# Attention, dense MLP and routed experts in one kernel: the routing's constants set up in eight pieces, and new pace numbers for the list that orders the work

## The chip, the cores and the metric

The kernel runs on one core of a Trainium2 chip. The metric is the device time of one execution in microseconds (us); less is better. Three executions of the kernel before took 875.04, 875.09 and 876.19 us, the median is 875.09 us.

## What is computed

The reference has three layers in a row, all in float32:

```python
# 1: attention with random features, 4 x 8 heads, 576 positions, 64 wide, 128 features
q_p, k_p = phi(q_s), phi(k_s)       # exp(x omega^T - |x|^2/2 - max) / sqrt(m)
kv, z = einsum('bhsm,bhsd->bhmd', k_p, v), sum(k_p, axis=2)
attn = (q_p @ kv) / (q_p @ z + 1e-6)
# 2: dense MLP, 2304 tokens x 512, hidden 2048
h = x @ w_in
x = (h - tanh(h)) @ w_out
# 3: eight experts, each token to one expert, at most 288 tokens an expert
logits = x @ w_gate                 # greedy assignment in order of the logits
out[mask] = maximum(x[mask] @ w1[e], 0) @ w2[e]
```

## The kernel before, in words

**Tiling.** The 2304 tokens are six blocks of 384. The dense MLP goes block by block; a block has 16 chunks of 128 hidden columns. A chunk is twelve matmuls into one PSUM bank (`chunk_ops`, L608 to L610: high and low parts of the float32 numbers multiplied in three products), a Square of the bank into `u` (L612, ScalarE), the polynomial for h - tanh(h) (L632 on ScalarE, L633 and L635 on VectorE), the split into high and low parts (`hidden_ops`, L303 and L308), and nine matmuls with the second weight matrix (`m2_ops`, L655). The ring of `u` has one buffer, that of the PSUM banks four.

**Attention** is cut into units (`unit_ops`): projections on TensorE (L433), a maximum on VectorE (L447), exponentials on ScalarE (L444), then either the sum over positions (L464) or the product with it (L486, L493, L506). 18 units run ahead of the MLP, the other 54 are spread over the first four blocks. `x_ops` (L548 to L556, and helpers L303 and L308) turns a finished token tile into the MLP's operand.

**Weights** come as 64-bit floats. `weight_ops` loads one 128 x 512 piece (L337, SyncE queue), takes it apart into a float32 in three VectorE operations (L338, L340, L342), rounds it to the high part on ScalarE, subtracts for the low part on GpSimd or VectorE (`low`, L308) and stores the low part in HBM (L351). There are 16 pieces of the first matrix ("wi") and 16 of the second ("wo"); the MLP loads the low parts again (`split_ops`, L569, tiles iL and oL, three buffers each).

**What sets the order.** All operations are handed to a planner (`Plan`) while the program is built. Each has an engine, a duration as the list believes it, the operations that it depends on, buffers of rings, and a due time (`plan.at` plus a lag). The planner plays the program through in its own time: of all that is ready it issues what can begin first, and among what can begin at the same time what is due first. So each engine gets its instructions in one fixed order. Due times, unless an operation is marked `early=False`, hold nothing back; they only decide between things that compete. An operation on the engine "-" costs the list nothing and runs its Python function when it is its turn: whatever instructions that function emits stand in the engines' queues at that place.

The due times come from a few pace numbers: T_MLP (due time of the first chunk), SB and SU (a block's length is SB plus SU for each attention unit in it), DUE0 and DUE1 (how far after the block's start its first attention unit is due, and how much of its end is left without), WI0, WI1 and WO0 (pieces of the weights), LEADX, LEADI and LEADO (how far ahead the MLP's operand and the two low parts are due). `low_ops` prepares low parts of the experts' weights in the fifth block with a pace of its own.

**The routing's constants** are made by `r_setup` (L956 to L1026): 14 index patterns by iota on GpSimd (L962 and L1002) and 31 short operations on VectorE (L972 to L1025). They are used only after the fifth block, by the routing. Before, one "-" operation emits all of them once the first chunk's Square (`flags[:1]`) has been issued.

Two small transfers, the zero row of the MLP's output (L1487) and the gate's weights (L1490), are on the SyncE queue near the start.

Of the kernel before, what the change touches and what calls it, by code (L numbers as in the profile page):

```python
# [8 lines left out]
F32 = mybir.dt.float32  # L9
# [180 lines left out]
def tile_kernel(ctx, tc, q, k, v, omega, w_in, w_out, w_gate, w_gate_t, w1, w2, out, dbg=None):  # L190
    nc = tc.nc
# [4 lines left out]
    P = 128  # L196
# [5 lines left out]
    NF = DFF // P  # L202
    E = w_gate.shape[1]
    BLK = 384
    NBLK = NT // BLK
    TPB = BLK // P
# [25 lines left out]
    ms = dram.tile([NT + 1, DM], F32, name="ms")  # L232
# [14 lines left out]
    wg = consts.tile([P, NC, P // NC], F32, name="wg")  # L247
# [19 lines left out]
    plan = Plan()  # L267
# [44 lines left out]
    bwg = Buf(None)  # L312
# [16 lines left out]
    def weight_ops(kind, f, rings, masked=None):  # L329
        raw, w, lw = (Buf(r) for r in rings)  # L330
        if kind == "wo" and not masked:
# [3 lines left out]
        V = nc.vector  # L335
        bits = lambda: w.t.bitcast(U32)
        plan.op(SP, 0.47, lambda e: nc.sync.dma_start(pair(raw), src64[kind][f]), w=[raw], nbytes=P * DM * 8)  # L337
        plan.op(DVE, 0.52, lambda e: V.tensor_scalar(  # L338
            bits(), raw.t[:, :, 1], 5, 2, op0=OP.logical_shift_left, op1=OP.logical_shift_right), r=[raw], w=[w], lag=5.0)
        plan.op(DVE, 0.66, lambda e: V.scalar_tensor_tensor(  # L340
            bits(), raw.t[:, :, 1], 0xC0000000, bits(), op0=OP.bitwise_and, op1=OP.bitwise_or), r=[raw, w], w=[w], lag=5.4)
        plan.op(DVE, 0.73, lambda e: V.scalar_tensor_tensor(  # L342
            bits(), raw.t[:, :, 0], 29, bits(), op0=OP.logical_shift_right, op1=OP.bitwise_or), r=[raw, w], w=[w], lag=6.0)
# [426 lines left out]
    HINT = NBLK * NF - 6  # L770
    LAG2, LEADX, LEADI, LEADO = 10.4, 15, 5.43, 4.91

    def mlp_ops(start, step, general=False):
# [4 lines left out]
        for j in range(NBLK - 1):  # L778
            for i in range(j, j + 1 if j < NBLK - 2 else NBLK):
                x[i] = Buf(xHr), Buf(xLr)  # L780
                for t in range(TPB):
                    plan.at = start[j] + (3.0 if i > j else -LEADX) + 1.5 * t
                    if i == j > 0 and not general:
                        plan.at = max(x_due[i * TPB + t] + 9.0, start[j - 1] + LEADX)
                    x_ops(i, t, *x[i], general)
# [170 lines left out]
    def r_setup():  # L956
# [3 lines left out]
        def iota(name, shape, pattern, base=0, cm=0):  # L960
            x = c.tile(shape, I32, name=name)
            nc.gpsimd.iota(x, pattern=pattern, base=base, channel_multiplier=cm)  # L962
            return x
# [3 lines left out]
        for i, wd in enumerate(WIDTH):  # L967
# [5 lines left out]
            t["bits"].append((x, n, sh))  # L973

        x, n, sh = t["bits"][0]
        f0 = c.tile([P, n], I32, name="thr0")
# [4 lines left out]
        nc.vector.tensor_tensor(f0, f0, z, op=OP.bitwise_xor)  # L981
        t["thr0"] = f0
        de = iota("dei", [P, E], [[-1, E]], base=E)
        t["desc"] = c.tile([P, E], F32, name="desc")
# [4 lines left out]
        nc.vector.tensor_copy(flat(t["jid"]), ji)  # L989

        pi = iota("pi", [P, 1], [[0, 1]], cm=1)
        pd = c.tile([P, 2], I32, name="pdig")
# [4 lines left out]
        nc.vector.tensor_copy(pf[:, 1:3], pd)  # L997
        nc.vector.tensor_scalar(pf[:, 3:4], pd[:, 1:2], 1.0 - P, float(P), op0=OP.mult, op1=OP.add)
        t["tri"] = c.tile([P, P], BF16, name="tri")
        nc.vector.tensor_scalar(t["tri"], jp, 0.0, None, op0=OP.is_gt)  # L1000
        sp = jp
        nc.gpsimd.iota(sp, pattern=[[0, P // LO], [1, LO]], base=0, channel_multiplier=0)  # L1002
        t["spread"] = c.tile([P, P], BF16, name="spread")
        nc.vector.tensor_scalar(t["spread"], sp, pf[:, 1:2], pf[:, 3:4], op0=OP.is_equal, op1=OP.mult)
        hm = iota("hmi", [P, NHI], [[1, NHI]])
        nc.vector.tensor_scalar(hm, hm, P // LO - 1, None, op0=OP.bitwise_and)
        t["hm"] = c.tile([P, NHI], F32, name="hm")
        nc.vector.tensor_scalar(t["hm"], hm, pf[:, 2:3], None, op0=OP.is_equal)
        t["rsel"] = c.tile([P, NG * P // LO], F32, name="rsel")
        nc.vector.memset(t["rsel"], 0.0)  # L1010
# [8 lines left out]
        nc.vector.memset(t["mfull"], 0.0)  # L1019
        nc.vector.memset(t["mfull"][:1], -1.0e6)  # L1020
        t["id8"] = c.tile([P, E], BF16, name="id8")
        nc.vector.tensor_copy(t["id8"], ident[:, :E])
        for name, n in (("d8", 1), ("r1", NHI)):
            t[name] = Buf(None, c.tile([P, n], BF16, name=name))
            nc.vector.memset(t[name].t, 0.0)  # L1025
        rt.update(t)  # L1026

    rings = {}
# [457 lines left out]
    plan.op(POOL, 0.3, lambda e: nc.gpsimd.memset(zero.t[:1].bitcast(F32), 0.0), w=[zero])  # L1486
    plan.op(SP, 0.47, lambda e: nc.sync.dma_start(ms[:1, :], zero.t[:1].bitcast(F32)), r=[zero])  # L1487
    plan.at = 30.0
    plan.op(POOL, 0.1, lambda e: nc.gpsimd.memset(wg, 0.0), w=[bwg])
    plan.op(SP, 0.47, lambda e: nc.sync.dma_start(wg[:, :, :E], w_gate.rearrange("(c p) e -> p c e", p=P)), w=[bwg])  # L1490
    units = attn_units()
    NEARLY = 18
    T_UNIT, T_MLP, DUE0, DUE1 = 2.2, 68.1, 4, 20


    SB, SU = 40.5, 1.95
    along = [16, 14, 14, 10, 0]
# [7 lines left out]
    for i, u in enumerate(units):  # L1505
        plan.at = due[i]
        unit_ops(*u, early=i < NEARLY)
        if i == NEARLY - 1:
            early_ops = plan.ops[n0:]
    WI0, WI1, WO0 = 4.51, 3.28, -1.5  # L1510
    for f in range(NF):
# [29 lines left out]

    low_ops(starts[-2], (NF * steps[-1] - 8.0) / (E * NPRE))
    plan.at = T_MLP
# [8 lines left out]
    plan.at = T_MLP + 100.0  # L1552
    plan.op("-", 0.0, lambda e: r_setup(), after=flags[:1])
    plan.op("-", 0.0, lambda e: tc.mark_branch_hint_location(
# [143 lines left out]
```

## Time and profile before

| | |
|---|---|
| median of three executions | 875.09 us |
| time of the profiled execution | 876.29 us |
| its span, first to last instruction | 874.5 us |
| around the span | 1.8 us |
| TensorE busy | 845.2 us (97% of the span) |
| VectorE busy | 652.2 us (75%) |
| ScalarE busy | 468.4 us (54%) |
| GpSimd busy | 247.0 us (28%) |
| mean granted clock of TensorE | 0.99 |

The profile shows one execution. Attention ahead of the MLP fills the first 50 us; the six MLP blocks follow up to some 535 us, then routing and experts. A wait of an engine is given with the work that ended it. The granted clock is 1.00 at 2.4 GHz and 0.50 at 1.2 GHz. TensorE's ends are modelled, so 100% busy doesn't say that every matmul ran at its shortest.

### The profile page before, as it was taken

To read this page: it belongs to the slowest core of one execution; us is meant where nothing else is said; L and a number is where in the kernel's file an instruction comes from. 1 tells how busy PE (TensorE), PEld (TensorE's weight loads), DVE (VectorE), ACT (ScalarE), POOL (GpSimd) and SP (SyncE) were. 2 spreads that over 40 slices of the span, in tenths; PEclk is the share of its full clock that TensorE was granted. 3 is DMA by queue.
4 is the path that set the end of the run, shared out by engine and by line. 5 is a ranking of instruction groups with operands and counts; after the bars stand their busy time and mean duration, and the time that the engine had idled before them with its cause. 6 is when DMAs were issued, how large, how long until landed. Compare 5 with 4: busy or idle time off the path is not lost. (4 is left out here: it accounts for less than half of the span.)

```text
span 874.5 us, 17508 instructions
## 1 busy us (share of the span) xinstructions
PE 845.2 (97%) x6158; PEld 754.0 (86%) x6158; DVE 652.2 (75%) x1933; ACT 468.4 (54%) x1018; POOL 247.0 (28%) x271
## 2 busy tenths in 40 slices
PE   8989999999999999999999998999999999999995
PEld 6878888888888888898988985777999999999995
DVE  5897999886677888797888866446887878877520
ACT  5875565654456554655457853014465555555621
POOL 1232433223352344344431024010132232231211
PEclk9999999999999999999999999999999999999998
DMA  8997878987457665743469874577889879779500
GB/s 248 330 299 245 281 239 264 291 273 240 126 177 215 183 198 190 240 125 109 134 213 335 278 257 155 172 246 252 262 204 295 277 200 277 264 182 339 199 28 28
DMA packets 103789, 193.94 MB, mean 222 GB/s; under 512 B 28305, under 2 KB 42257, under 8 KB 103698
## 3 DMA queue, kind: packets, MB, share of 16 engines
q1 hardware_dynamic: 98034, 173.92, 60.7%
q0 software_dynamic: 5664, 18.88, 9.0%
q8 instruction: 49, 0.80, 0.4%
q14 instruction: 42, 0.34, 0.1%
HBM read 149.64 MB, written 33.69 MB: 210 GB/s over the span
## 5 line engine op out<-in xcount | busy, mean ns | idle before, releaser
L608 PE MATMUL bk<-xH,wi 128*128 128x384 f32 x332 | 118.7, 358 | 1.9 <-DVE xt L506 1.1
L736 DVE SCALAR_TENSOR_TENSOR lw<-wf,raw 128x512 f32<-128x512 f32 x128 | 108.6, 848 | 5.4 <-POOL wf L733 4.0
L609 PE MATMUL bk<-xL,wi 128*128 128x384 f32 x332 | 112.1, 338 | 0.5 <-DVE xL L308 0.5
L610 PE MATMUL bk<-xH,iL 128*128 128x384 f32 x332 | 112.2, 338 | 0.0
L655 PE MATMUL acc<-wo,gL 128*128 128x512 f32 x282 | 111.2, 395 | 0.0
L308 POOL TENSOR_TENSOR gL<-s,gH 128x384 fp32r<-128x384 f32 x49 | 58.8, 1200 | 145.9 <-ACT gH L303 143.5
L655 PE MATMUL acc<-wo,gH 128*128 128x512 f32 x240 | 99.4, 415 | 0.0
L444 ACT ACTIVATE phi<-bk,nm 128x128 f32<-128x128 f32 x272 | 77.2, 384 | 35.4 <-DVE nm L447 35.0
L655 PE MATMUL acc<-oL,gH 128*128 128x512 f32 x240 | 95.0, 396 | 0.3 <-DVE oL L308 0.3
L733 POOL TENSOR_TENSOR wf<-oL,wo 128x512 f32<-128x512 f32 x48 | 66.6, 1389 | 64.5 <-DMA oL<-low_wo 54.3
L303 ACT ACTIVATE gH<-s 128x384 fp32r<-128x384 f32 x80 | 42.0, 525 | 62.5 <-DVE s L635 43.4
L633 DVE SCALAR_TENSOR_TENSOR s<-s,bk 128x384 f32<-128x384 f32 x83 | 45.5, 549 | 35.5 <-ACT s L632 35.2
L608 PEld LDWEIGHTS bk<-xH,wi 128*128 128x128 f32 x332 | 63.0, 190 | 9.8 <-issue 2.0
L609 PEld LDWEIGHTS bk<-xL,wi 128*128 128x128 f32 x332 | 63.1, 190 | 3.2 <-DVE xL L308 0.7
L655 PEld LDWEIGHTS acc<-wo,gL 128*128 128x128 f32 x282 | 53.0, 188 | 12.5 <-POOL gL L308 0.4
L612 ACT ACTIVATE u<-bk 128x384 f32<-128x384 f32 x80 | 39.2, 490 | 44.8 <-PE bk L610 43.3
L610 PEld LDWEIGHTS bk<-xH,iL 128*128 128x128 f32 x332 | 62.7, 189 | 0.0
L447 DVE TENSOR_REDUCE nm<-bk 128x4 f32<-128x512 f32 (+1 forms) x75 | 46.3, 631 | 10.7 <-PE bk L433 9.2
L635 DVE SCALAR_TENSOR_TENSOR s<-s,u 128x384 f32<-128x384 f32 x80 | 51.8, 648 | 1.3
L632 ACT ACTIVATE s<-u,qbias 128x384 f32<-128x384 f32 x80 | 49.4, 617 | 4.9 <-DVE gL L308 3.2
L655 PEld LDWEIGHTS acc<-wo,gH 128*128 128x128 f32 x240 | 45.2, 188 | 7.2 <-ACT xm L303 0.4
L655 PEld LDWEIGHTS acc<-oL,gH 128*128 128x128 f32 x240 | 45.2, 188 | 6.1 <-DVE oL L308 0.6
(417 smaller groups left out, 2325.1 us busy)
## 6 DMA issues: line engine op xcount, KB each, us to landing
r_wraw<-in_moe_w_dram SPq DMA_DIRECT2D x50, 512.0 KB
iL<-low_wi SPq DMA_DIRECT2D x80, 256.0 KB
oL<-low_wo SPq DMA_DIRECT2D x78, 256.0 KB
raw<-in_moe_w_in_dram SPq DMA_DIRECT2D x32, 512.0 KB
raw<-in_moe_w_out_dram SPq DMA_DIRECT2D x32, 512.0 KB
s_wraw<-in_moe_w_dram SPq DMA_DIRECT2D x14, 512.0 KB
dw<-in_moe_w_dram SPq DMA_DIRECT2D x13, 512.0 KB
w1l<-dw SPq DMA_DIRECT2D x13, 512.0 KB
```

What stands on the lines that cost most here:

```text
L308: (nc.gpsimd if e == POOL else nc.vector).tensor_tensor(out, in_, high.bitcast(F32), op=OP.subtract)
L444: nc.scalar.activation(ph.t[:, i0 + i, :], pj.t[:, i * M:(i + 1) * M], AF.Exp, bias=nmx.t[:, i0 + i:i0 + i + 1])
L447: plan.op(DVE, 0.1 + 0.125 * n, lambda e, pj=pj, i0=i0, n=n: V.tensor_reduce(nmx.t[:, i0:i0 + n], pj.t[:, :n * M].rearrange("p (i m) -> p ...
L608: nc.tensor.matmul(ph(), piece(iH, c), xH.t[:, c, :], start=(c == 0), stop=False)
L609: nc.tensor.matmul(ph(), piece(iH, c), xL.t[:, c, :], start=False, stop=False)
L610: nc.tensor.matmul(ph(), piece(iL, c), xH.t[:, c, :], start=False, stop=(c == NC - 1))
L632: plan.op(ACT, 0.52, lambda e: nc.scalar.activation(s.t, ut(), AF.Square, bias=qbias), r=[u], w=[s], lag=2.8)
L633: plan.op(DVE, 0.52, lambda e: V.scalar_tensor_tensor(s.t, s.t, QD, ph(), op0=OP.add, op1=OP.mult), r=[p, s], w=[s], lag=3.4)
L635: plan.op(DVE, 0.65, lambda e: V.scalar_tensor_tensor(s.t, s.t, QC, ut(), op0=OP.mult, op1=OP.mult), r=[u, s], w=[s], lag=4.0)
L655: nc.tensor.matmul(acc[t].t, (gL if k == 2 else gH).t[:, c], (oL if k == 1 else oH).t, start=(f == 0 and k == 0), stop=(f == end and k == ...
L733: plan.op(POOL, 1.45, lambda e: nc.gpsimd.tensor_tensor(w.t, lo.t.bitcast(F32), wo[:, f, :].bitcast(F32), op=OP.add), r=[lo, wbuf["wo", f] ...
L736: x_reads.append(plan.op(DVE, 0.9, lambda e, i=i: nc.vector.scalar_tensor_tensor(scratch.t.bitcast(F32), w.t, 1.0, half(rows[i // 2], i % ...
```

## The change

`r_setup` becomes a generator with eight yields. In place of the one "-" operation there are eight operations on VectorE, each believed to take 0.5 us, each after the one before it and after the Square of one of chunks 24 to 31 (the second half of the second block). Three durations of the conversion and the pace numbers get other values, and the two small transfers are not issued before their due times (60 and 30 us of the list's time).

```diff
 def weight_ops(...)
-        plan.op(DVE, 0.52, lambda e: V.tensor_scalar(
+        plan.op(DVE, 0.5, lambda e: V.tensor_scalar(
...
-        plan.op(DVE, 0.66, lambda e: V.scalar_tensor_tensor(
+        plan.op(DVE, 0.78, lambda e: V.scalar_tensor_tensor(
...
-        plan.op(DVE, 0.73, lambda e: V.scalar_tensor_tensor(
+        plan.op(DVE, 0.75, lambda e: V.scalar_tensor_tensor(
...
-    LAG2, LEADX, LEADI, LEADO = 10.4, 15, 5.43, 4.91
+    LAG2, LEADX, LEADI, LEADO = 10.4, 16.22, 0.85, 5.03
...
-                        plan.at = max(x_due[i * TPB + t] + 9.0, start[j - 1] + LEADX)
+                        plan.at = max(x_due[i * TPB + t] + 9.4, start[j - 1] + LEADX)
...
 def r_setup():
     (seven of the eight yields stand between these parts, the last at the end:)
     bits | thr0 | desc, i16, i18, jid | pf | tri, iota into jp | spread, hm | rsel to mfull | id8, d8, r1
...
-    plan.op(SP, 0.47, lambda e: nc.sync.dma_start(ms[:1, :], zero.t[:1].bitcast(F32)), r=[zero])
+    plan.op(SP, 0.47, lambda e: nc.sync.dma_start(ms[:1, :], zero.t[:1].bitcast(F32)), r=[zero], early=False)
...
-    plan.op(SP, 0.47, lambda e: nc.sync.dma_start(wg[:, :, :E], w_gate...), w=[bwg])
+    plan.op(SP, 0.47, lambda e: nc.sync.dma_start(wg[:, :, :E], w_gate...), w=[bwg], early=False)
...
-    T_UNIT, T_MLP, DUE0, DUE1 = 2.2, 68.1, 4, 20
-    SB, SU = 40.5, 1.95
+    T_UNIT, T_MLP, DUE0, DUE1 = 2.2, 78.63, 3.94, 32.79
+    SB, SU = 42.26, 1.7
...
-    WI0, WI1, WO0 = 4.51, 3.28, -1.5
+    WI0, WI1, WO0 = 4.51, 3.98, -1.13
...
-    low_ops(starts[-2], (NF * steps[-1] - 8.0) / (E * NPRE))
+    low_ops(starts[-2], (NF * steps[-1] + -10.57) / (E * NPRE))
...
-    plan.op("-", 0.0, lambda e: r_setup(), after=flags[:1])
+    setup, o = r_setup(), []
+    for i in range(8):
+        o = [plan.op(DVE, 0.5, lambda e: next(setup), after=flags[NF + NF // 2 + i:][:1] + o)]
```

## Rows read from the trace of the kernel before

**Rows 1.** Busy time by stage: stretch, its length, busy us (instructions), clock, DMA share, GB/s.
```profile
core 0: us, PE busy (x) PEld busy (x) DVE busy (x) ACT busy (x) POOL busy (x), PEclk, DMA share, GB/s
0.00:110.00 110.00, 98.03 (x814) 86.47 (x814) 92.04 (x219) 72.57 (x203) 28.75 (x52) 0.97 0.88 280
110.00:440.00 330.00, 329.74 (x2137) 289.72 (x2136) 269.35 (x628) 182.40 (x438) 126.50 (x103) 1.00 0.64 200
200.00:250.00 50.00, 50.00 (x309) 44.66 (x308) 31.56 (x75) 23.49 (x57) 18.74 (x18) 1.00 0.57 165
420.00:440.00 20.00, 20.00 (x107) 18.25 (x106) 17.27 (x41) 7.88 (x17) 9.89 (x7) 1.00 0.48 137
```

**Rows 2.** Busy time by stage, same columns, from 58.5 to 69.2 us.
```profile
58.50:61.60 3.10, 0.01 (x1) 0.00 (x0) 3.10 (x8) 2.96 (x8) 1.10 (x1) 1.00 0.94 292
61.60:65.80 4.20, 4.16 (x32) 3.94 (x33) 4.20 (x8) 3.20 (x11) 1.00 (x1) 0.59 0.80 255
65.80:69.20 3.40, 3.40 (x13) 3.40 (x12) 1.57 (x3) 1.30 (x6) 0.00 (x0) 0.50 0.45 175
```

**Rows 3.** Timeline of TensorE: start us, us, instruction, count, idle time before and its releaser.
```profile
56.19 1.00 PE L464 MATMUL kv<-v,phi 128*128 128x65 f32 x8
...
61.64 1.41 PE L433 MATMUL bk<-omT,ld 64*128 64x128 f32 x14 [3.13 <-DVE s L633]
62.97 1.97 PE L464 MATMUL kv<-v,phi 128*128 128x65 f32 x8
...
66.98 0.52 PE L608 MATMUL bk<-xH,wi 128*128 128x384 f32 x1
```

**Rows 4.** Timeline of VectorE: the constants' first and last row, and the two L633.
```profile
53.49 0.66 DVE L972 TENSOR_SCALAR tb<-tb 128x31 int32<-128x31 int32 x7
...
56.84 0.07 DVE L1025 MEMSET r<- 128x9 uint32 x1
57.42 0.54 DVE L633 SCALAR_TENSOR_TENSOR s<-s,bk 128x384 f32<-128x384 f32 x1
...
61.04 0.54 DVE L633 SCALAR_TENSOR_TENSOR s<-s,bk 128x384 f32<-128x384 f32 x1
```

**Rows 5.** Timeline of ScalarE: the first chunk's operation ahead of L633.
```profile
54.83 0.62 ACT L632 ACTIVATE s<-u,qbias 128x384 f32<-128x384 f32 x1
```

**Rows 6.** Waits of TensorE from 60 to 120 us: in total, times, longest (us).
```profile
PE bk L608 <- DVE xt L506: 1.1, 1, 1.1
PE bk L493 <- ACT qt L303: 1.0, 1, 1.0
```

**Rows 7.** Timeline of ScalarE: Squares of chunks 24, 27, 30 and 31.
```profile
206.15 0.49 ACT L612 ACTIVATE u<-bk 128x384 f32<-128x384 f32 x1 [1.68 <-PE bk L610]
...
226.96 0.49 ACT L612 ACTIVATE u<-bk 128x384 f32<-128x384 f32 x1 [1.17 <-PE bk L610]
...
242.17 0.49 ACT L612 ACTIVATE u<-bk 128x384 f32<-128x384 f32 x1 [1.24 <-PE bk L610]
246.35 0.49 ACT L612 ACTIVATE u<-bk 128x384 f32<-128x384 f32 x1 [1.22 <-PE bk L610]
```

**Rows 8.** Timeline of GpSimd: one of its subtractions.
```profile
145.00 1.40 POOL L308 TENSOR_TENSOR oL<-wf,wo 128x512 fp32r<-128x512 f32 x1 [2.70 <-DMA low_wo<-oL]
```

**Rows 9.** Groups by line, VectorE, 0 to 155 us: count, busy us, mean ns, idle before.
```profile
L342 DVE SCALAR_TENSOR_TENSOR wf<-raw,wf 128x512 uint32<-128x512 uint32 x32 | 26.7, 833 | 0.2
L340 DVE SCALAR_TENSOR_TENSOR wf<-raw,wf 128x512 uint32<-128x512 uint32 x32 | 26.5, 828 | 0.2
...
L338 DVE TENSOR_SCALAR wf<-raw 128x512 uint32<-128x512 uint32 x32 | 17.0, 531 | 2.5 <-DMA raw<-in_moe_w_in_dram 1.9 <-POOL lw L308 0.5
```

**Rows 10.** Timeline of the SyncE queue: the load of chunk 30's low part.
```profile
226.89 0.34 SPq L569 DMA_DIRECT2D iL<-low_wi  x1
```

**Rows 11.** Timeline of TensorE: a wait for a load near the start.
```profile
11.86 0.37 PE L433 MATMUL rx<-omT,ld 64*128 64x128 f32 x1 [1.29 <-DMA ld<-in_k_dram]
```

**Rows 12.** Busy time by stage: two late chunks of the first block, columns as in the first group.
```profile
143.30:151.70 8.40, 8.40 (x44) 7.58 (x43) 7.84 (x13) 3.39 (x7) 2.92 (x3) 1.00 0.91 287
```

**Rows 13.** Groups by line, VectorE, 115 to 141 us: a low part subtracted on VectorE.
```profile
L308 DVE TENSOR_TENSOR oL<-wf,wo 128x512 fp32r<-128x512 f32 x2 | 2.0, 976 | 0.0
```

**Rows 14.** Timeline of VectorE: a polynomial step beside the subtraction on GpSimd.
```profile
145.18 1.65 DVE L635 SCALAR_TENSOR_TENSOR s<-s,u 128x384 f32<-128x384 f32 x1
```

More of the change, by code (lines that the diff above doesn't have):

```diff
@@ L973, in r_setup @@
             t["bits"].append((x, n, sh))
+        yield
         x, n, sh = t["bits"][0]
@@ L982, in r_setup @@
         t["thr0"] = f0
+        yield
         de = iota("dei", [P, E], [[-1, E]], base=E)
@@ L989, in r_setup @@
         nc.vector.tensor_copy(flat(t["jid"]), ji)
+        yield
         pi = iota("pi", [P, 1], [[0, 1]], cm=1)
@@ L998, in r_setup @@
         nc.vector.tensor_scalar(pf[:, 3:4], pd[:, 1:2], 1.0 - P, float(P), op0=OP.mult, op1=OP.add)
+        yield
         t["tri"] = c.tile([P, P], BF16, name="tri")
@@ L1002, in r_setup @@
         nc.gpsimd.iota(sp, pattern=[[0, P // LO], [1, LO]], base=0, channel_multiplier=0)
+        yield
         t["spread"] = c.tile([P, P], BF16, name="spread")
@@ L1008, in r_setup @@
         nc.vector.tensor_scalar(t["hm"], hm, pf[:, 2:3], None, op0=OP.is_equal)
+        yield
         t["rsel"] = c.tile([P, NG * P // LO], F32, name="rsel")
@@ L1020, in r_setup @@
         nc.vector.memset(t["mfull"][:1], -1.0e6)
+        yield
         t["id8"] = c.tile([P, E], BF16, name="id8")
@@ L1026, in r_setup @@
         rt.update(t)
+        yield
     rings = {}
@@ L1486, in tile_kernel @@
     plan.op(POOL, 0.3, lambda e: nc.gpsimd.memset(zero.t[:1].bitcast(F32), 0.0), w=[zero])
-    plan.op(SP, 0.47, lambda e: nc.sync.dma_start(ms[:1, :], zero.t[:1].bitcast(F32)), r=[zero])
+    plan.op(SP, 0.47, lambda e: nc.sync.dma_start(ms[:1, :], zero.t[:1].bitcast(F32)), r=[zero], early=False)
     plan.at = 30.0
     plan.op(POOL, 0.1, lambda e: nc.gpsimd.memset(wg, 0.0), w=[bwg])
-    plan.op(SP, 0.47, lambda e: nc.sync.dma_start(wg[:, :, :E], w_gate.rearrange("(c p) e -> p c e", p=P)), w=[bwg])
+    plan.op(SP, 0.47, lambda e: nc.sync.dma_start(wg[:, :, :E], w_gate.rearrange("(c p) e -> p c e", p=P)), w=[bwg],
+            early=False)
     units = attn_units()
     NEARLY = 18
-    T_UNIT, T_MLP, DUE0, DUE1 = 2.2, 68.1, 4, 20
-    SB, SU = 40.5, 1.95
+    T_UNIT, T_MLP, DUE0, DUE1 = 2.2, 78.63, 3.94, 32.79
+    SB, SU = 42.26, 1.7
     along = [16, 14, 14, 10, 0]
```

## The prediction

> **What bounds the kernel now.** I read the busy time by stage first. From 110 to 440 us TensorE is busy for 329.74 of 330.00 us at full clock [rows 1]: these blocks are its work and nothing else, and what a new order does there can only lose. The first 110 us are another matter: TensorE is idle for 110.00 - 98.03 = 11.97 us, the mean clock is 0.97, VectorE is busy for 92.04 us and the DMA engines for 0.88 of the time [rows 1]. There is the room for a gain.
>
> The same view in finer steps shows where most of it lies. From 58.50 to 61.60 us TensorE does nothing, while VectorE and ScalarE are busy throughout. Behind that the granted clock is 0.59 for 4.20 us and 0.50 for 3.40 us, the lower of its two levels, though TensorE is then at work nearly all the time [rows 2]. The reader should see a stall that costs twice.
>
> The timelines say who makes it. TensorE's wait of 3.13 us ends with L633 on VectorE [rows 3]. On VectorE the routing's constants run from 53.49 to 56.91 us, 3.42 us in one piece, in the middle of the first chunk [rows 4]. ScalarE has the first chunk's polynomial ready at 54.83 + 0.62 = 55.45 us [rows 5]; L633, which takes it, starts at 57.42 [rows 4]. The rest follows in order: u has one buffer, so the second chunk's Square comes behind the first chunk's L635, the second L633 starts only at 61.04 [rows 4], it frees a PSUM bank, and TensorE goes on at 61.64.
>
> **The change part by part.**
>
> *The constants move.* 31 VectorE operations and 14 iotas leave 50 to 57 us. L633 of the first chunk could start at 55.45 instead of 57.42, about 1.9 us earlier once the usual hand-over is taken off, and the chain behind it shifts by as much. The stall of 3.10 us shrinks to some 1.2. Bounds: nothing gained if another wait steps in, all 3.10 if the conversions ahead of L633 also move up. I take 1.9, because that is what the chain itself gives.
>
> *The clock.* Waits of 1.29, 1.1 and 1.0 us [rows 11, 6] are not followed by a lower clock; the fall stands behind the one of 3.10. So I expect none behind 1.2 us. What it cost in work: eight L464 matmuls took 1.97 us instead of 1.00 [rows 3], 0.97 us; and the 3.40 us at 0.50, filled with the third chunk's matmuls such as the L608 at 66.98 [rows 2, 3], are 1.70 us too long. Together 2.67. The bounds are 0 (it falls all the same) and 0.41 x 4.20 + 0.50 x 3.40 = 3.42 us (every throttled cycle was needed). The lower sum is nearer, since part of 61.6 to 65.8 is work that only fills time.
>
> The Trainium skill ("TensorE: Matmul & The Clock Gate", section "Terms") has a plain rule for this: the penalty is about the throttled time multiplied by the share of clock withheld. By it the clock would give back 3.4 us and the sum below would be 5.3 rather than 4.6; it counts time in which TensorE had little to do, so the count of the rows is kept.
>
> *Where the constants go.* Each of eight pieces stands behind the Square of one of chunks 24 to 31, at 206.15 to 246.35 us now [rows 7]. VectorE is busy there for 31.56 of 50.00 us [rows 1]; 3.42 us more is 35 of 50, so the cover is 18 us and the price 0. Five pieces hold iotas, and a VectorE operation that needs one waits for GpSimd's queue, with the polynomial steps queued behind it: at most one GpSimd operation of 1.40 us [rows 8] each, 5 x 1.40 = 7 us of VectorE time, still inside the 18. If the cover were gone, the bank of the chunk would be late and the price at most 3.42 + 7.0 us; I take 0.
>
> *Three durations.* The list will believe 2.03 us for a piece of weights instead of 1.91; measured means are 0.531 + 0.828 + 0.833 = 2.19 [rows 9]. No instruction changes. It brings the list closer to the chip, 32 x 0.12 = 3.8 us of VectorE time that it did not plan for before. I price it at 0, with the bounds of the next item.
>
> *Pace numbers.* T_MLP moves 10.5 us later with SB and SU nearly the same, and the first matrix's pieces are due later too (the last at 64.2 rather than 53.7), so the 18 early attention units gain precedence over conversions on VectorE. DUE1 moves each block's attention units into its first half. That changes only who goes first. The bounds come from the rows: at best the other idle time of the first 110 us, 11.97 - 3.10 = 8.9; at worst the rival of the first block's second half, below. I take 0, the middle of something that I can't order by hand.
>
> *Loads.* LEADI makes the low parts due 4.6 us later, LEADO 0.1 us earlier. Chunk 30's load goes out at 226.89 [rows 10], with chunk 27's Square at 226.96 [rows 7]: it is sent when a buffer comes free, not when it is due, and 15 us ahead of its own Square at 242.17. Price 0; cover gone, it would be a late chunk, which the 0.26 us of idle time in 330 [rows 1] doesn't show anywhere. The low part of the experts' weights in the fifth block gets 0.01 us a step more: 0.
>
> *The two small transfers* leave the start of the SyncE queue for their due times. The one early wait for a load is 1.29 us [rows 11], which is the most that they could give; what they pass over are the loads of attention and weights. They cost an issue each later on. I take 0.
>
> **The sum.** 1.9 + 2.7 = 4.6 us off the profiled execution: 876.29 - 4.6 = 871.7. That execution lies 1.2 us above the median of the runs, 875.09, and so the prediction is 875.09 - 4.6 = 870.5 us. Its own range goes from the gain of 1.9 (873.2) to 3.10 + 3.42 = 6.5 (868.6).
>
> **The rivals.**
>
> *A: another wait takes the stall's place.* VectorE is busy all through 58.50 to 65.80 us [rows 2], so without the constants its queue is full of conversions instead, u still has one buffer, and the clock may fall as before. For it: VectorE does 92 of 110 us there. Against it: L633 is held by nothing but queue order. About 1 us is left of the gain: 874.1.
>
> *B: slower, by the first block's second half.* With DUE1 at 32.79 of a block of 42.26 + 16 x 1.7 = 69.46, some eight chunks have no attention beside them, while the second matrix's conversions go on. TensorE needs 246.35 - 242.17 = 4.18 us for a chunk alone [rows 7]. In two such chunks VectorE is busy for 7.84 of 8.40 us, 3.92 a chunk, with GpSimd taking the low parts [rows 12]. If VectorE takes them, it is 3.92 + 0.98 = 4.90 [rows 13], which is 0.72 x 8 = 5.8 us too much, and if the idle time gathers as it does now, one fall of the clock adds 2.7: 875.09 + 8.5 - 4.6 = 879.0. With that fall it decides from 4.18 + (4.6 + 1.75 - 2.7) / 8 = 4.64 us a chunk. For it: L635 took 1.65 us [rows 14], begun 0.18 us after a GpSimd subtraction of 1.40 [rows 8], against some 0.55 elsewhere. Against it: TensorE was busy for all of those 8.40 us. The Trainium skill ("SBUF — State Buffer", section "Who interferes with whom") says that a VectorE instruction with two SBUF inputs blocks until a GpSimd instruction that reads SBUF is done, if that began first; the trace agrees, 146.40 plus 0.5 is where that L635 ends. It speaks against packing conversions and polynomial steps closer, as the new DUE1 does.
>
> *C: more is gained.* The waits of 1.0 and 1.1 us [rows 6] also come from VectorE and ScalarE running late behind the stall; with 3.42 us less in their queue they go too: 4.6 + 2.1 = 6.7, 868.4, at most 3.10 + 3.42 + 2.1 = 8.6, 866.5.
>
> *D: the change doesn't do what it says*: the pieces would be issued early, since nothing but the Squares holds them. But each is tied to a Square, and these to their matmuls; I give it no chance of its own.
>
> **How the numbers follow.** A measurement of this kernel can tell about 0.2% from no change, 1.75 us. Forecast 0.50, C 0.15, A 0.16, B 0.19. Faster is the forecast and C, 0.65; the same is A, 0.16; slower is B, 0.19. The range runs from C's far end, 866.5, to 877.0, part of the way to B: outside lie some 0.05 below and 0.15 above.
>
> **What would show it.** In the changed profile: no VectorE rows of L972 to L1025's kind before 200 us, and eight groups of them in the second block's second half with TensorE still at 20.00 of 20.00 us there; no idle stretch over 2 us between 50 and 70 us, and the clock 1.00 throughout the first 110 us; chunks of the first block's second half about 4.2 us apart. Wrong would be: a new TensorE wait for VectorE of 2 us or more in the first 110 us, a second fall of the clock, chunks 8 to 15 spaced by 4.6 us or more without attention between them, or a wait for iL.

## The result and the profile after

The changed kernel takes 881.5 us against 875.07 us before, medians of fourteen executions each. One execution of each, disturbed (923.58 and 1024.73 us), counts in these medians but neither in the ratio nor in the table of clocks below. The ratio is 1.0063, with a 95% interval of 1.0034 to 1.0091. The changed kernel is slower, by some 5.5 us. Forecast was 870.5, faster.

Busy time by stage in the profile of the changed kernel (880.77 us, span 879.0), with the columns of [rows 1]:

```profile
core 0: us, PE busy (x) PEld busy (x) DVE busy (x) ACT busy (x) POOL busy (x), PEclk, DMA share, GB/s
0.00:110.00 110.00, 97.49 (x790) 87.32 (x791) 83.73 (x177) 69.72 (x199) 20.85 (x34) 0.91 0.87 262
110.00:440.00 330.00, 329.78 (x2136) 289.63 (x2134) 277.30 (x650) 179.75 (x433) 136.19 (x121) 1.00 0.64 203
219.80:258.00 38.20, 38.20 (x208) 34.22 (x207) 33.36 (x90) 15.85 (x33) 20.88 (x30) 1.00 0.55 161
...
20.00:21.80 1.80, 0.85 (x8) 0.88 (x8) 1.80 (x4) 1.80 (x7) 0.00 (x0) 0.97 1.00 345
21.80:32.00 10.20, 10.20 (x63) 9.53 (x64) 6.50 (x13) 6.26 (x23) 0.23 (x2) 0.50 1.02 323
69.60:72.20 2.60, 0.18 (x4) 0.10 (x1) 2.60 (x5) 1.44 (x3) 1.62 (x1) 1.00 0.83 262
72.20:82.40 10.20, 10.18 (x55) 9.84 (x55) 4.48 (x9) 3.13 (x11) 1.38 (x2) 0.53 0.68 204
```

The long middle is as full as before [rows 1]. The first 110 us differ: about as much idle time (110.00 - 97.49 = 12.51 us, before 11.97), but a clock of 0.91 instead of 0.97. TensorE now runs at half clock for 10.2 us from 21.8 us on and for some 10 us again from 72.9 us on, where before it was 6.8 us once [rows 2]. Clock withheld (the length of a stretch multiplied by one minus its clock) over the 110 us is 0.09 x 110 = 9.9 us against 0.03 x 110 = 3.3: 6.6 us more.

How far each kernel is at a given time is read from ScalarE's Squares (L612). These are the first of the third and of the fifth block, before and then after. At each of the two places both kernels have done nearly the same work: all weights are converted, and the attention's last step (L506) has run 41 and 40 times at the first, 73 and 72 at the second.

```profile
250.75 0.49 ACT L612 ACTIVATE u<-bk 128x384 f32<-128x384 f32 x1 [0.60 <-PE bk L610]
...
440.36 0.47 ACT L612 ACTIVATE u<-bk 128x384 f32<-128x384 f32 x1
```

```profile
258.00 0.47 ACT L612 ACTIVATE u<-bk 128x384 f32<-128x384 f32 x1
...
449.41 0.47 ACT L612 ACTIVATE u<-bk 128x384 f32<-128x384 f32 x1
```

So 7.25 us are lost by the start of the third block and 9.05 by that of the fifth. The last Square comes at 535.78 us instead of 530.45, 5.3 us late: the last two blocks give 3.7 us back. The loss of some 5.5 us is thus what is left of a larger loss and a gain. (The last Square isn't yet the end of the MLP: matmuls with its second matrix, L655, follow up to 608 us in the kernel before, and not to some 535 as the overview has it.)

TensorE's timeline shows what stands ahead of each fall of the clock:

```profile
20.95 2.96 PE L464 MATMUL kv<-v,phi 128*128 128x65 f32 x16 [1.34 <-ACT phi L444]
...
72.22 1.55 PE L1486 MATMUL kv<-onev 128*128 128x128 bf16 x18 [2.44 <-DVE kvs L478]
```

The first fall is behind a wait of only 1.34 us, hardly longer than the 1.29 us that were harmless before [rows 11]. The second is behind one of 2.44 us, and the timelines of VectorE and then GpSimd tell how it came about:

```profile
69.61 0.55 DVE L635 SCALAR_TENSOR_TENSOR s<-s,u 128x384 f32<-128x384 f32 x1
70.08 1.76 DVE L342 SCALAR_TENSOR_TENSOR wf<-raw,wf 128x512 uint32<-128x512 uint32 x1
71.75 0.41 DVE L478 TENSOR_TENSOR kvs<-kvs,kv 128x260 f32<-128x260 f32 x1
```

```profile
69.66 1.62 POOL L308 TENSOR_TENSOR lw<-wf,wi 128x512 fp32r<-128x512 f32 x1 [0.80 <-DMA low_wi<-lw]
```

A conversion step (L342) that takes 0.69 us elsewhere in this stretch takes 1.76 beside a subtraction on GpSimd and ends behind it; the sum that frees the accumulator of the attention is queued behind the conversion, and TensorE waits for that. It is the same pattern as L635 in [rows 14], now on the path.

The constants are where the change puts them. Two rows of VectorE, L972 of the first piece and an operation of the sixth, and the GpSimd row beside the latter:

```profile
220.99 0.78 DVE L972 TENSOR_SCALAR tb<-tb 128x31 int32<-128x31 int32 x7 [1.51 <-POOL tb L962]
...
246.65 1.21 DVE L1011 TENSOR_SCALAR hmi<-hmi 128x18 int32<-128x18 int32 x1
```

```profile
246.55 1.28 POOL L733 TENSOR_TENSOR wf<-oL,wo 128x512 f32<-128x512 f32 x1
```

VectorE waits 1.51 us for the first iotas, and some short operations become long, yet TensorE is busy for 38.20 of 38.20 us there, so no wait of TensorE comes of it; that the pieces' price is 0 is shown by run 1 below.

**Time goes with the clock.** Each execution comes with its mean granted clock. For the changed kernel:

| us | 874.40 | 879.03 | 879.09 | 879.82 | 880.59 | 880.73 | 880.77 | 882.23 | 882.73 | 883.13 | 883.28 | 883.85 | 884.83 |
|---|---|---|---|---|---|---|---|---|---|---|---|---|---|
| clock | 0.991 | 0.986 | 0.986 | 0.985 | 0.982 | 0.984 | 0.982 | 0.983 | 0.979 | 0.979 | 0.981 | 0.981 | 0.980 |

Withheld clock (one minus the clock, times the execution's time) is 15.9 us in the median; a line through the points rises 0.84 us for each of these. The executions of the kernel before that stand in the result above have no clock on record. The 35 that ran beside experiments 5 to 8 have 9.7 us in the median and a rise of 0.89. So 6.2 us more are withheld, worth 5.2 to 5.5 us at these two rises. The rise is not well known: over the sets of executions of the other runs it goes from 0.60 to 0.97, and 6.2 us are then worth 3.7 to 6.0. In the net the loss is about as large as what the clock costs; other losses and gains beside it largely cancel, and the experiments below show some of them.

### The profile page after: what moved, and what is told of

The parts are those of the page before. It is cut to its first block, busy times and chain, and to the rows that moved or that the text cites. A ratio compares the mean times of both kernels' runs of the same rounds, so it can differ in the third digit from the quotient of the medians.

```text
span 879.0 us, 17525 instructions
## 1 busy us (share of the span) xinstructions
PE 850.8 (97%) x6169; PEld 761.4 (87%) x6169; DVE 659.8 (75%) x1930; ACT 466.2 (53%) x1017; POOL 255.5 (29%) x275
## 5 line engine op out<-in xcount | busy, mean ns | idle before, releaser
L308 POOL TENSOR_TENSOR gL<-s,gH 128x384 fp32r<-128x384 f32 x60 | 74.9, 1249 | 155.2 <-ACT gH L303 154.0
L655 PE MATMUL acc<-wo,gL 128*128 128x512 f32 x282 | 111.1, 395 | 0.0
L736 DVE SCALAR_TENSOR_TENSOR lw<-wf,raw 128x512 f32<-128x512 f32 x128 | 103.9, 812 | 2.4 <-POOL wf L733 1.0
L655 PE MATMUL acc<-wo,gH 128*128 128x512 f32 x240 | 99.2, 414 | 0.0
L655 PE MATMUL acc<-oL,gH 128*128 128x512 f32 x240 | 95.0, 396 | 0.0
L444 ACT ACTIVATE phi<-bk,nm 128x128 f32<-128x128 f32 x264 | 75.1, 378 | 29.8 <-DVE nm L447 29.5
L733 POOL TENSOR_TENSOR wf<-oL,wo 128x512 f32<-128x512 f32 x48 | 68.7, 1432 | 59.1 <-DMA oL<-low_wo 53.1
L633 DVE SCALAR_TENSOR_TENSOR s<-s,bk 128x384 f32<-128x384 f32 x83 | 45.4, 548 | 26.7 <-ACT s L632 26.4
L655 PEld LDWEIGHTS acc<-wo,gL 128*128 128x128 f32 x282 | 52.9, 188 | 12.1
L612 ACT ACTIVATE u<-bk 128x384 f32<-128x384 f32 x80 | 38.8, 485 | 43.2 <-PE bk L610 40.1
L635 DVE SCALAR_TENSOR_TENSOR s<-s,u 128x384 f32<-128x384 f32 x80 | 59.5, 744 | 1.0
L655 PEld LDWEIGHTS acc<-wo,gH 128*128 128x128 f32 x240 | 45.1, 188 | 7.2 <-issue 0.3
L655 PEld LDWEIGHTS acc<-oL,gH 128*128 128x128 f32 x240 | 45.2, 188 | 6.0 <-DMA oL<-low_wo 0.2
```

Of the source, the lines that this page charges most:

```text
L308: (nc.gpsimd if e == POOL else nc.vector).tensor_tensor(out, in_, high.bitcast(F32), op=OP.subtract)
L444: nc.scalar.activation(ph.t[:, i0 + i, :], pj.t[:, i * M:(i + 1) * M], AF.Exp, bias=nmx.t[:, i0 + i:i0 + i + 1])
L633: plan.op(DVE, 0.52, lambda e: V.scalar_tensor_tensor(s.t, s.t, QD, ph(), op0=OP.add, op1=OP.mult), r=[p, s], w=[s], lag=3.4)
L635: plan.op(DVE, 0.65, lambda e: V.scalar_tensor_tensor(s.t, s.t, QC, ut(), op0=OP.mult, op1=OP.mult), r=[u, s], w=[s], lag=4.0)
L655: nc.tensor.matmul(acc[t].t, (gL if k == 2 else gH).t[:, c], (oL if k == 1 else oH).t, start=(f == 0 and k == 0), stop=(f == end and k == ...
L733: plan.op(POOL, 1.45, lambda e: nc.gpsimd.tensor_tensor(w.t, lo.t.bitcast(F32), wo[:, f, :].bitcast(F32), op=OP.add), r=[lo, wbuf["wo", f] ...
```

## The experiments

Each ran beside the kernel before on one chip; the ratio is to that kernel. Short names: pieces (the constants in eight), durations, WI (WI1 and WO0), crowding (DUE0 and DUE1), rest (T_MLP, SB, SU, the leads with the 9.4, the fifth block's pace, the two small transfers). The changed kernel is all five. Half clock and the times of Squares are quoted from one profile each. The runs were made on three chips, 1 to 4 and 13 to 16 on one, 5 to 8 on a second, 9 to 12 on a third; the kernel before took 878.4, 877.8 and 873.5 us there, and 878.6 beside the last four.

**1. The pieces alone.**

```diff
-    plan.op("-", 0.0, lambda e: r_setup(), after=flags[:1])
+    setup, o = r_setup(), []
+    for i in range(8):
+        o = [plan.op(DVE, 0.5, lambda e: next(setup), after=flags[NF + NF // 2 + i:][:1] + o)]
...  (and the eight yields of r_setup)
```

> The kernel before with the constants in eight pieces and nothing else; up to chunk 26 TensorE's order is the same as before. Theory 1 (the loss is made in the first 80 us by the new pace numbers, which starve TensorE more finely and let its clock fall for longer; the pieces themselves help): the stall of 3.10 us at 58.5 us shrinks below 2, 870 to 873 us. Theory 2 (the pieces cost more in the second block than they give back in the first): 877 to 881 us, with chunks 24 to 31 later than before by 3 us or more. Theory 3 (falls of the clock come by chance and both kernels are alike): within 2 us of the kernel before.

0.9977 (0.9959 to 0.9995), medians 874.81 and 878.35. Faster, by 2.0 us by the ratio and 3.5 by the medians, and the clock's median goes from 0.989 to 0.9925. Theory 1 has the sign and the stall, but not its 870 to 873 us; theory 3, within 2 us, is at the edge of the ratio. The stall in its profile, on TensorE and then VectorE:

```profile
59.18 1.16 PE L433 MATMUL bk<-omT,ld 64*128 64x128 f32 x14 [1.41 <-DVE s L633]
```

```profile
54.76 0.55 DVE L633 SCALAR_TENSOR_TENSOR s<-s,bk 128x384 f32<-128x384 f32 x1 [1.18 <-ACT s L632]
...
58.59 0.54 DVE L633 SCALAR_TENSOR_TENSOR s<-s,bk 128x384 f32<-128x384 f32 x1
```

L633 starts as soon as ScalarE is done, the second one 2.45 us earlier than in [rows 4], the wait is 1.41 us instead of 3.13, and the clock stays at 1.00 for the whole 110 us:

```profile
0.00:110.00 110.00, 99.82 (x830) 86.99 (x831) 94.68 (x195) 74.66 (x209) 29.95 (x40) 1.00 0.92 291
```

The Squares of chunks 16, 24 and 32 begin at 151.73, 202.17 and 246.77 us, where before it was 155.71, 206.15 and 250.75: 3.98 us earlier at each of the three. So in these two profiles the move gains 4.0 us by the second block, and the pieces, which stand between the last two, cost nothing. The last Square is still 4.2 us early (526.22 against 530.45).

**2. All but the pieces.**

```diff
-    setup, o = r_setup(), []
-    for i in range(8):
-        o = [plan.op(DVE, 0.5, lambda e: next(setup), after=flags[NF + NF // 2 + i:][:1] + o)]
+    plan.op("-", 0.0, lambda e: r_setup(), after=flags[:1])
...  (and r_setup without its yields)
```

> The changed kernel with the constants in one place again, behind the first chunk's Square; TensorE's order is that of the changed kernel to the last row. Theory 1: the early loss of the changed kernel stays and the constants add their own, 882 to 886 us, with the clock at half for 15 us or more of the first 90. Theory 2: the constants' cost in the second block is gone, 874 to 877 us. Theory 3: within 2 us of the kernel before, 873 to 877 us.

1.0128 (1.0092 to 1.0164), clock 0.9815. The median, 887.6 us, is above the 882 to 886 of theory 1, and theory 2 falls in both runs. TensorE's order is that of the changed kernel, so by the ratios the pieces are worth 1.0128 - 1.0063 = 0.65%, 5.7 us, inside it, though the two intervals all but touch. The profile doesn't show it: its last Square is at 535.32 us, that of the changed kernel at 535.78, but the profiled execution (883.91 us) is one of the fastest of this run. It has half clock early as well, from 11.9 to 22.1 us, where the changed kernel, with the same order, has full clock up to 21.7; three of these microseconds:

```profile
17.00:20.00 3.00, 3.00 (x21) 2.88 (x22) 0.68 (x3) 1.14 (x3) 1.33 (x2) 0.50 0.70 221
```

**3 and 4. More filling work**, in the changed kernel and in the one before.

```diff
-            if e == "PE" and self.fill and t - self.free[e] > 0.9:
-                self.fill(min(0.4 * (t - self.free[e]), 1.0))
+            if e == "PE" and self.fill and t - self.free[e] > 0.3:
+                self.fill(min(0.75 * (t - self.free[e]), 2.5))
```

> The changed kernel with more filling work for TensorE ahead of the second weight matrix's end: the planner puts small matmuls into gaps of its own time from 0.3 us on instead of 0.9, 0.75 of the gap instead of 0.4, 112 of them instead of 53. Theory 1: the clock falls less or not at all in the first 90 us, and 10 us at half less give back 3 to 5 us each: 873 to 878 us. Theory 2: no gain, the filling work delays real work by up to 3 us: 881 to 884 us. Theory 3: no change beyond chance.

> The kernel before with the same filling work as the run above, 110 small matmuls instead of 42 or so. Theory 1: its one early fall of the clock, 6.8 us at half, goes or shortens: 869 to 874 us. Theories 2 and 3: 875 to 878 us, the filling work gains nothing.

1.0073 (1.0048 to 1.0098) with a clock of 0.990, and 1.0019 (0.9992 to 1.0045) with 0.991. The clock rises in the changed kernel, from 0.982, and the time does not fall: what the clock gives back by more small matmuls doesn't show in the time. Theory 1's numbers were missed in both runs; the medians, 884.78 and 880.27 us, are above those of theory 2, on a chip where the kernel before is 3 us slower too. What the falls cost can't be had back in this way.

**5 to 8. The pieces with one group each.**

In short, each on top of run 1:

```
+durations 0.5, 0.78, 0.75                         (5)
+WI1, WO0 = 3.98, -1.13                            (6)
+DUE0, DUE1 = 3.94, 32.79                          (7)
+the rest                                          (8)
```

> The kernel before with the constants in pieces (0.9977 of before by itself) and the three new conversion durations, nothing else. TensorE's order differs from the row of the ninth attention projections on, ahead of the first chunk. If the durations make the falls of the clock: 1.003 to 1.010 of the kernel before, mean clock 0.985 or less, with half clock ahead of 40 us in the profile. If another edit does: 0.996 to 1.000, clock 0.990 or more.

> The kernel before with the constants in pieces and the new WI1 and WO0 alone, which make the conversions due later than the early attention units. If conversions late against attention starve TensorE: 1.003 or more of the kernel before with a clock of 0.985 or less. If another edit does: 0.996 to 1.000.

> The kernel before with the constants in pieces and the new DUE0 and DUE1 alone, which crowd each block's attention units into its first half; nothing differs ahead of the third chunk. If that makes the loss, either by waits of TensorE and a fall of the clock between 60 and 90 us or by second halves of the blocks that VectorE bounds: 1.003 or more of the kernel before; the rival forecast as slower priced the second halves at 5.8 us. If another edit does: 0.996 to 1.000.

> The kernel before with the constants in pieces and all the other edits: T_MLP, SB, SU, LEADX, LEADI, LEADO, the 9.4, the fifth block's pace, and the two small transfers held to their due times. TensorE's order is unchanged up to the eighth chunk. If the early falls of the clock are what the change costs, none is added here: 0.995 to 1.000. If these make the loss: 1.003 or more.

Durations 0.9993 (0.9961 to 1.0025), WI 1.0020 (0.9989 to 1.0052), crowding 1.0067 (1.0036 to 1.0098), rest 0.9933 (0.9895 to 0.9971). Median clocks are 0.9905, 0.983, 0.988 and 0.9925. Run 6 has the clock that was expected of a loss, but its ratio lies between its two ranges; run 8 is faster than its range. WI loses by the clock: its line of time over withheld clock gives 875.7 us where 8 us are withheld, the pieces alone 875.8. Crowding doesn't: 883.1 at the same 8 us. (Run 1 was on another chip than these, with nearly the same time of the kernel before, 878.35 and 877.81.) And the rest with the pieces is the best version so far, faster than both kernels. Where it gains is seen in the profiles. The fifth and sixth block, from the first Square of the fifth (437.29 us) to the last Square (523.96), take 86.7 us in run 8 and 89.8 in run 1. They take 86.4 to 87.4 in all nine profiles with the rest and 89.6 to 93.0 in all eight without it (run 12, with the leads alone, has 88.3). Up to the fifth block run 8 is no faster than run 1 (437.29 against 436.41).

**9. The changed kernel without the crowding.**

```diff
-    T_UNIT, T_MLP, DUE0, DUE1 = 2.2, 78.63, 3.94, 32.79
+    T_UNIT, T_MLP, DUE0, DUE1 = 2.2, 78.63, 4, 20
```

> The changed kernel with DUE0 and DUE1 as before (4 and 20) and all else changed. Theory: the crowding of attention units is the largest part of the loss, 0.7 to 0.9%, whatever stands around it; then 0.995 to 1.000 of the kernel before. Rival: the loss is made by the edits together, WI1's falls of the clock above all; then 1.002 to 1.006.

1.0123 (1.0092 to 1.0153): slower yet, against both expectations. The early fall is there (half clock from 21.6 us for some 10 us), and a new stretch of waits stands behind 130 us. TensorE's waits from 130 to 215 us:

```profile
PE bk L486 <- ACT phi L444: 2.3, 2, 2.0
PE acc L655 <- DVE oL L308: 1.7, 2, 0.9
PE bk L608 <- DVE xL L308: 1.0, 1, 1.0
```

TensorE is busy for 98.36 of the 105 us from 110 to 215 there, in the changed kernel for 104.84. So the edits don't add up: each set makes an order of its own, with its own waits.

**10 and 11. The crowding in parts**, on the pieces alone.

```diff
+        d0, d1 = (3.94, 32.79) if j == 0 else (DUE0, DUE1)      (10; 11 has j > 0)
```

> The kernel before with the constants in pieces and the new DUE0 and DUE1 for the first block alone; TensorE's order is that of the run with the new DUE everywhere up to chunk 19. Theory: the loss is made between chunks 2 and 10 of the first block, where units crowd while weights are still converted: 1.003 to 1.007 of the kernel before. Rival: it is spread over all four blocks' second halves, which VectorE bounds: 0.998 to 1.001.

> The kernel before with the constants in pieces and the new DUE0 and DUE1 for the second to fourth block alone. Theory: little is lost there, 0.997 to 1.001 of the kernel before. Rival: the loss is spread over the blocks' second halves, 1.003 or more.

1.0072 (1.0041 to 1.0104) and 1.0070 (1.0045 to 1.0095), where both parts together gave 1.0067. Either part loses 0.9% against the pieces alone, and together they lose no more. The theory that only the first block loses is wrong. In the second of these the order up to chunk 19 is that of the pieces alone, so what the order loses is lost behind some 160 us. The stretch from 110 to 440 us there:

```profile
110.00:440.00 330.00, 328.21 (x2122) 287.21 (x2121) 278.06 (x649) 179.00 (x431) 134.83 (x121) 1.00 0.63 198
```

That is 1.79 us of idle time where the pieces alone have none, with VectorE a little busier; it doesn't account for all of the 8 us. The Squares show where the two parts lose. Run 10 is 10.1 us behind run 1 at the start of the third block (256.90 against 246.77) and no more than 10.6 at the last Square: the first block's crowding is paid for in the first two blocks. Run 11 is 2.6 us late at the start of the second block, where its order is still that of run 1 and its clock has fallen by chance, 3.3 at the third, 6.9 at the fifth and 10.1 at the last Square. Run 7, with both, is 8.9 us late at the third block and 13.0 at the last Square, so in the profiles the parts do add up to some extent; the ratios don't show it.

**12. The pieces with the leads and the small transfers.**

```diff
+    LAG2, LEADX, LEADI, LEADO = 10.4, 16.22, 0.85, 5.03     (and 9.4, and early=False twice)
```

> The kernel before with the constants in pieces, the new LEADX, LEADI, LEADO and 9.4, and the two small transfers held to their due times. The run with all the remaining edits was 0.9933 of the kernel before, the pieces alone 0.9977. If these leads make the difference: 0.992 to 0.995. If the pace of the blocks (T_MLP, SB, SU, the fifth block) does: 0.996 to 0.999.

0.9986 (0.9966 to 1.0005), like the pieces alone: leads and transfers do nothing that these runs can tell.

**13 to 16. Groups taken out of the changed kernel.**

In short, each taken back to its old value:

```
-WI1, WO0 = 3.98, -1.13                                     (13)
-WI1, WO0 = 3.98, -1.13 and the durations                   (14)
-the durations                                              (15)
-WI1, WO0 = 3.98, -1.13 and DUE0, DUE1 = 3.94, 32.79        (16)
```

> The changed kernel with WI1 and WO0 as before. In all four profiles so far in which the new durations and the new WI1 stood together, the clock was at half for 10.2 us ahead of 32 us; in nine of ten others it was not. Theory: the two together order the first 35 us so that TensorE is starved there; without WI1 the early fall goes, mean clock 0.986 or more, and 2 to 6 us come back: 1.000 to 1.004 of the kernel before. Rival: the falls come from the crowding, or from chance, and nothing changes: 1.005 to 1.008, clock 0.983 or less.

> The changed kernel with WI1, WO0 and the durations as before; what stays is the crowding (DUE0, DUE1) and the edits that gave 0.9933. Theory: no early fall, clock 0.987 or more, and what is left is the crowding's loss of 0.9% against 0.9933: 1.000 to 1.004. Rival: 1.005 or more.

> The changed kernel with the durations as before, WI1 and WO0 new. Theory (durations and WI1 together make the early fall): no fall ahead of 35 us, though WI1 alone had one from 57 us on; clock 0.984 to 0.988, 1.001 to 1.006. Rival (WI1 by itself makes the early fall): clock 0.982 or less and 1.006 or more.

> The changed kernel with WI1, WO0, DUE0 and DUE1 as before: the pieces, the durations and the edits that gave 0.9933. Up to chunk 10 TensorE's order is that of the pieces with the durations alone, 0.9993. Theory: no early fall, no crowding, 0.994 to 0.999 of the kernel before. Rival (every new set of pace numbers brings a stall of its own, as the run with DUE0 and DUE1 back did at 1.0123): 1.002 or more, with a new wait of TensorE behind 100 us.

Run 16 came as its theory had it. Run 13 has the theory's clock and the rival's time, run 14 its rival's ratio; run 15 missed both, being faster than either and with an early fall all the same. All have pieces and rest. With what else they have:

| beside pieces and rest | ratio | median clock |
|---|---|---|
| nothing (8) | 0.9933 | 0.9925 |
| durations (16) | 0.9959 (0.9933 to 0.9985) | 0.990 |
| crowding (14) | 1.0061 (1.0043 to 1.0079) | 0.9915 |
| durations, crowding (13) | 1.0051 (1.0025 to 1.0078) | 0.988 |
| WI, crowding (15) | 1.0005 (0.9985 to 1.0025) | 0.989 |
| durations, WI (9) | 1.0123 | 0.984 |
| durations, WI, crowding (the changed kernel) | 1.0063 | 0.982 |

Taking WI back mends the clock and not the time (13): the crowding then loses by itself. Taking the crowding back alone makes it worse (9). Taking both back gives a faster kernel (16). But taking back the durations alone, which cost next to nothing by themselves (5, 16), also ends the loss against the kernel before (15, 1.0005). And WI makes the kernel with the crowding faster (14 to 15) and that with the durations slower (16 to 9). So the loss belongs to no group: it belongs to the combination. WI beside pieces and rest alone was not run.

Half clock ahead of 32 us stands in six profiles, and at two places. In the changed kernel, 3 and 9 it begins at 21.6 to 22.3 us, behind the wait for ScalarE shown above (1.34, 0.90 and 1.30 us). In 2, 11 and 15 it begins at 11.9 to 13.5 us, behind a wait of 1.58, 1.03 and 1.27 us for a load, and waits of 1.29 us (the kernel before), 1.43 (9) and 1.11 (the changed kernel) for the same load have none behind them. Five of the six have WI, of six that have it; but 11 has at that place the very order of run 1, which shows no fall, and 2 that of the changed kernel, where the fall comes 10 us later. So the order makes a fall likelier at most, and chance takes part. The first place has been seen only with durations and WI together; why, is not shown.

What the crowding does to the first block is seen in 14 against 8. First 14, then 8: busy time from 62 to 122 us, and TensorE's longest waits from 62 to 126 us:

```profile
62.00:122.00 60.00, 52.57 (x360) 46.04 (x359) 52.95 (x103) 35.84 (x90) 16.57 (x13) 0.97 0.81 258
```

```profile
PE bk L608 <- DVE xt L506: 2.1, 2, 1.4
PE bk L433 <- DVE xt L506: 2.0, 1, 2.0
```

```profile
62.00:122.00 60.00, 55.47 (x366) 48.83 (x364) 54.69 (x99) 36.21 (x91) 20.03 (x17) 0.97 0.80 262
```

```profile
PE bk L608 <- DVE xt L506: 1.1, 1, 1.1
PE bk L486 <- ACT phi L444: 1.1, 1, 1.1
```

TensorE idles for 2.9 us more at the same clock, waiting longest for the attention's last step on VectorE (L506), while VectorE itself is busy for less: it is not short of time, it is at something else in its fixed order. For the wait of 2.0 us, VectorE's timeline and then GpSimd's in run 14 show at what:

```profile
72.45 1.76 DVE L342 SCALAR_TENSOR_TENSOR wf<-raw,wf 128x512 uint32<-128x512 uint32 x1
...
74.86 0.49 DVE L506 TENSOR_TENSOR xt<-bk,den 128x128 f32<-128x128 f32 x2
```

```profile
72.10 1.57 POOL L308 TENSOR_TENSOR lw<-wf,wi 128x512 fp32r<-128x512 f32 x1 [1.68 <-ACT qt L303]
```

It is the long conversion step again. By the start of the third block run 14 is 9.1 us behind run 8 (256.22 against 247.12). TensorE's idle time makes up 4.4 of these (15.69 against 11.30 us up to there); what makes the other 4.7, in which the profile has TensorE busy, is not shown.

## Why the prediction was wrong

**The constants' term was right in kind and somewhat too large.** The forecast had the stall shrink from 3.10 to about 1.2 us, and no fall of the clock behind it; run 1 shows 1.41 us and none. Forecast were 4.6 us, measured 0.23%, 2.0 us (0.4 to 3.6), with 3.5 by the medians and 4.0 up to the second block in the profile. Inside the changed kernel the same move is worth 5.7 us by the ratios. The price of 0 in the second block was right (3.98 us early before and behind the pieces), and so was the bound: iotas were waited for, and it was hidden.

**The step that failed is the one on pace numbers, priced at 0.** WI, crowding, durations and rest together cost 1.0063 - 0.9977 = 0.86%, 7.5 us. The argument was that they only change who goes first, and 0 was taken as the middle of two bounds, 8.9 us of gain and the rival's 5.8 of loss. The runs show that an order is all it takes: beside the pieces, 0.9933 with the rest alone, 1.0123 with the rest, WI and durations. Two of the zeros hid large terms of opposite sign: the crowding of the first block costs 9 to 10 us by the third block (runs 7 and 10 against 1, 14 against 8), and the rest gains 3.1 us in the fifth and sixth (run 8 against 1), where the forecast had put the new pace at 0 as well.

**The clock's step failed for the same stretch.** From waits of 1.0 to 1.3 us without a fall it was concluded that such waits are safe. A wait of 1.34 us at 19.6 us had 10.2 us of half clock behind it, one of 1.41 us in run 1 had none, and thirteen executions of one program run from 0.979 to 0.991. The length of a single wait doesn't decide it. What a withheld microsecond costs was not the error. The forecast's count, 2.67 us for 3.42 withheld, is 0.78; across executions it is 0.60 to 0.97 (0.84 for the changed kernel). The page "TensorE: Matmul & The Clock Gate" of the Trainium skill (section "Terms") puts the penalty at the throttled time multiplied by the share withheld, which makes it 1. All the sets of executions here lie below that, so in these runs it is an upper bound.

**Rival B had the sign, the edit and part of the mechanism**, the conversion step that is long beside a subtraction on GpSimd (the Trainium skill, "SBUF — State Buffer", section "Who interferes with whom": L342 with two SBUF inputs at 70.08 us in the changed kernel fits it, ending 0.56 us behind the GpSimd row that began first). Its place was wrong: not the first block's second half, bound by VectorE's time, but the first half, where units crowd, and the later blocks too (run 11). Its 879.0 us is near the 881.5 that came by luck, for the sum is another. (Its eight chunks without attention are nearer seven: the last unit is due 3.94 + 15/16 x 36.67 = 38.3 us into a block of 69.46, and a chunk takes 4.34 of the list's time.)

**Right at 0:** the leads and the small transfers (run 12), and the durations by themselves, 0.9993 with the pieces, an interval that holds 0.9977. Beside WI and crowding the durations are not 0: without them the changed kernel is at 1.0005 (run 15).

**Open.** Why crowding in the first block and crowding in the later ones cost 0.9% each and no more together by the ratios; what makes TensorE's busy time longer where units crowd; why WI helps beside the crowding and hurts beside the durations; and which edit of the rest shortens the last two blocks: the intervals of runs 1 and 8 overlap (0.9959 to 0.9971), so how much of 0.9933 is the rest's own isn't settled by the times alone.

## What to carry to other kernels

Setup work that is needed late should not stand in one piece in the queue of an engine that feeds a short chain of few buffers; small pieces where that engine has slack were free here, even though they got longer there. Pace numbers of a list schedule can't be priced one at a time: take them out in groups, in both directions, and count a new order as a risk on both sides. A net difference can be a loss in one stage and a gain in another, so compare the times at which both kernels reach the same work. Where a program sits at the edge of a clock gate, look at the clock of every execution before a difference is put down to waits.

## What the runs showed of the hardware

Among the falls looked at here, half clock stood behind waits of TensorE of 0.90 us (run 3) to 3.13 us (the kernel before), while a wait of 1.43 us (run 9, for a load) had none behind it; and it did not always come at the same place for the same order. Filling matmuls raised the clock from 0.982 to 0.990 and saved nothing. Behind the last Square of the MLP the rest of the kernel took 345.3 to 349.6 us in the eight profiles of one chip, 343.7 to 344.9 in the four of a second and 340.2 to 342.2 in the four of a third, so totals of different chips are compared only as ratios. And very small VectorE operations suffer beside GpSimd like large ones: L1011, 18 columns, took 1.21 us begun 0.10 us behind a GpSimd subtraction of 1.28 us, where the same operation (L1006 in the kernel before, at 55.95 us) took 0.17 us with GpSimd idle.
